# Turning the rows of an eight-expert layer by 16-bit transfers in place of matrix transposes

## The chip, the cores and the metric

The kernel runs on one core of a Trainium2 chip. A core has a matrix engine (TensorE; PE in the profile, PEld for its weight loads), VectorE (DVE), ScalarE (ACT), GpSimd (POOL) and SyncE (SP), which here only issues transfers. Each engine works through its own list of instructions in order; semaphores tie the lists together. Sixteen DMA engines move data for all of them. SBUF is the memory of 128 partitions that the engines work in, PSUM the memory that TensorE writes to. The metric is the device time of one execution in microseconds; lower is better.

## The reference

Two stages. The first is a recurrent attention with a decay per channel (4 batches, 8 heads, 768 steps, head width 48); its result is laid out as 3072 rows (tokens) of 384 channels. The second sends each row to one of eight experts, the one with the largest logit, and scales the expert's answer by its softmax weight:

```python
state = alpha[:, :, t, :, None] * state + np.einsum('bhd,bhe->bhde', k[:, :, t], v[:, :, t])
y[:, :, t] = np.einsum('bhd,bhde->bhe', q[:, :, t], state)
...
expert_idx = np.argmax(logits, axis=1)
...
h = np.maximum(x_sorted[lo:hi] @ w1[e], 0.0)      # 384 -> 1024
y_sorted[lo:hi] = h @ w2[e]                       # 1024 -> 384
...
return (gate_w[:, None] * y).astype(np.float32)
```

Everything is 32-bit floating point.

## The kernel before

**First half.** Attention runs in 24 tiles of 128 steps (6 chunks of 4 batches), in a loop written out by hand: the order of the calls in the loop over `i` (L669 to L743) is the order of the instructions on each engine. GpSimd forms the scaled keys and queries of tile `i + 2` (`operands`, L433; its output `kqb` has three buffers), carries the decay of a chunk's end to its rows (`decay_rows`, L414, tile `er`), multiplies the carried state by it (`scale_state`, L471, tile `U`) and makes some of the one-hot rows that route tokens (`one_hots`, L288). TensorE turns `er` into columns (`decay_cols`, L427), VectorE copies them (`E`, L431), and `scale_state` waits for that. TensorE's `read_state` (L480) waits for `U`. The finished rows go to a buffer `x_rows` in device memory. At `i = 21` TensorE counts the one-hots of 16 tiles together into `tok` (`tokens`, L296).

**Second half.** The experts are ordered by how many rows they have; place 0 has the most. Places have fixed capacities: 424 - 8i rows for place i, of which place 0 has 256 done early, within the first half's end. So the rows per place are 168, 416, 408, 400, 392, 384, 376, 368, in blocks of 128: 2, 4, 4, 4, 4, 3, 3, 3. For each place:

- `gather` (L787): one indirect transfer per block, issued by GpSimd, brings rows into `xg` (rows on partitions; two buffers).
- `turn` (L795): three TensorE transposes per block into PSUM (`tp`), and a copy by VectorE or ScalarE into `xgT` (channels on partitions). `row_sums` (L805) forms sums of halves on VectorE into `t1`.
- `layer1` (L863): 384 channels into 1024, by a scheme of Strassen's kind on the first two thirds of the channels: seven products P1 to P7 in place of eight, with the last third of the channels (R11, R12, R22, Rd) added plainly. It runs over four tiles `a`; `chain` (L816) holds the parts `p1`, `p2`, `p7`, `p6`, `p5`, `c22`, `p34`. P1, P6, P5 and P3 are added one after another onto one PSUM bank A, and between two of them ScalarE copies the bank out (`keep`: `p1`, `u2`, `u4`; `p` and `u` in the profile). The next product on A therefore waits for that copy. VectorE's adds and ScalarE's relus form `h`; VectorE forms sums of `h` in `th`. The third and fourth product of a tile run late, within the next tile, ahead of its fifth.
- `layer2` (L924): 1024 into 384 with the same chain, four matmuls to a product; the last third of the output channels is done plainly with eight matmuls of the full row count (L957). The results lie in `zT`, channels on partitions.
- `rows_out` (L988): three TensorE transposes per block and a ScalarE copy into `zo` (`scatter`, L972), then an indirect transfer by GpSimd to the output rows. It is a generator; `layer1` of the next place takes one block of it per tile (`next(rows, None)`, L917).

The loop over the places (L1153) sets the order: `layer1` with the previous place's results beside it; `begin`, the first product of layer 2; then the fetch of a later place's `w1` on SP, the gather of place `i + 2`, and `rest` (L953) with `between`, the generator that turns the next place's rows in two steps. The fetch of a later `w2` follows. On SP the fetches wait until the weight buffer that they overwrite has been read (two buffers). The instruction order on each engine is the program's order here too. The last place has no transposed results: `rows_layer2` (L998) leaves rows on partitions.

Of the kernel before, what the change touches and what calls it, by code (L numbers as in the profile page):

```python
# [10 lines left out]
I32 = mybir.dt.int32  # L11
AX = mybir.AxisListType.X
# [6 lines left out]
def kernel(  # L19
# [29 lines left out]
    nc = tc.nc  # L49
# [313 lines left out]
    with tc.tile_pool(name="ld", bufs=6) as ld, \  # L363
# [305 lines left out]
        for i in range(-4, NT):  # L669
# [114 lines left out]
    def blocks(g):  # L784
        return [(j, min(C, g["n"] - j * C)) for j in range(-(-g["n"] // C))]

    def gather(g):  # L787
        g["xg"] = xg_pool.tile([C, NJ, Dm], F32, name="xg")
        for j, r in blocks(g):
# [5 lines left out]
    def turn(g):  # L795
        g["xT"] = wk.tile([C, DB, CAP0], F32, name="xgT")
# [7 lines left out]

    def row_sums(g):  # L805
        m = g["n"] // 2
        g["t1"] = wk.tile([C, 5, CAP0 // 2], F32, name="t1")
# [8 lines left out]
    def chain(g, terms, out, res):  # L816
# [37 lines left out]
        def p34():  # L854
            terms(bank["A"][:, :m], False, "P3", "R12")
            res(0, 1, bank["A"][:, :m])
            terms(bank["B"][:, :m], False, "P4", "Rd")
# [3 lines left out]
        return p1, p2, p7, p6, p5, c22, p34  # L861

    def layer1(g, rows, ahead, last):  # L863
# [57 lines left out]
        ahead()  # L921
        prev()

    def layer2(g):  # L924
        n, m = g["n"], g["n"] // 2
        w2, h, s, t = g["w2"], g["h"], g["s2"], g["th"]
        g["zT"] = wk.tile([C, DB, CAP0], F32, name="zT")
# [23 lines left out]
        p1, p2, p7, p6, p5, c22, p34 = chain(g, terms, out, res)  # L951

        def rest(ahead, between):  # L953
            p2()
            d2 = mps.tile([C, 512], F32, name="pC", tag="pC")
            for f in range(FB):
                nc.tensor.matmul(  # L957
                    d2[:, :n], lhsT=w2[:, f, 2 * C :], rhs=h[:, f, :n], start=(f == 0), stop=(f == FB - 1),
                )
            ahead()  # L960
            p6()
            nc.scalar.copy(z[:, 2, :n], d2[:, :n])
# [9 lines left out]
    def scatter(g, j, r, zp, shared=False):  # L972
        zo = wk.tile([C, Dm], F32, name="zo", bufs=3)
# [3 lines left out]
        else:  # L977
            nc.scalar.copy(zo[:r], zp)  # L978
        ins = nc.gpsimd.indirect_dma_start(  # L979
# [8 lines left out]
    def rows_out(g):  # L988
        for j, r in blocks(g):
            zp = mps.tile([C, DB, C], F32, name="tp", tag="tp")  # L990
            for a in range(DB):
                nc.tensor.transpose(zp[:r, a, :], g["zT"][:, a, j * C : j * C + r], ident[:])
# [266 lines left out]
```

## Time and profile before

| | |
|---|---|
| median of 23 runs | 416.78 us (415.71 to 418.3) |
| the profiled execution: time | 416.86 us |
| its span, first to last instruction | 415.0 us |
| granted TensorE clock, mean | 0.997 |
| first half, about | 0 to 157 us |
| place 0, about | 157 to 182 us |
| place 3, both layers, about | 249.5 to 282.7 us: TensorE busy 33.1, VectorE 17.3, ScalarE 12.0, GpSimd 7.8 us |
| the last place and the end, about | 378 to 415 us |

The span is what the trace covers; the time of the execution has 1.86 us more around it. In the profile a matrix transpose is a MATMUL with the identity (`ident`) as an input. One matmul of 32-bit data is recorded as two MATMUL records, one transpose as one. Matmuls are pipelined: the durations overlap, and what one costs is seen from the starts of its successors. A line number after L is that of the kernel before. In the groups by line each row gives line, engine, operation, output and inputs, shape, count, then busy time, the mean duration in ns, and the idle time of the engine just ahead, with what ended it.

### The profile page before, as it was taken

To read this page: it belongs to the slowest core of one execution; us is meant where nothing else is said; L and a number is where in the kernel's file an instruction comes from. 1 tells how busy PE (TensorE), PEld (TensorE's weight loads), DVE (VectorE), ACT (ScalarE), POOL (GpSimd) and SP (SyncE) were. 2 spreads that over 40 slices of the span, in tenths; PEclk is the share of its full clock that TensorE was granted. 3 is DMA by queue.
4 is the path that set the end of the run, shared out by engine and by line. 5 is a ranking of instruction groups with operands and counts; after the bars stand their busy time and mean duration, and the time that the engine had idled before them with its cause. 6 is when DMAs were issued, how large, how long until landed. Compare 5 with 4: busy or idle time off the path is not lost.

```text
span 415.0 us, 9238 instructions
## 1 busy us (share of the span) xinstructions
PE 403.6 (97%) x3525; PEld 340.7 (82%) x3525; DVE 213.1 (51%) x644; ACT 170.6 (41%) x453; POOL 143.7 (35%) x193
## 2 busy tenths in 40 slices
PE   7999999999998999999999999999999999999995
PEld 4677888888887875999699889979979979979952
DVE  5545545665567574645833663463573573553200
ACT  4575555565654530134125314513513523523510
POOL 5555464596758105604002501310330230200101
PEclk9999999999999999999999999999999999999998
DMA  8999999999863217764405335155154153200101
GB/s 171 201 206 216 200 215 197 214 205 225 195 180 118 80 39 263 250 238 125 154 6 186 102 132 171 50 201 172 39 210 148 62 207 122 85 1 21 35 19 36
DMA packets 120098, 59.08 MB, mean 142 GB/s; under 512 B 102934, under 2 KB 114287, under 8 KB 120052
## 3 DMA queue, kind: packets, MB, share of 16 engines
q1 hardware_dynamic: 114932, 48.80, 44.8%
q0 software_dynamic: 3424, 9.59, 6.7%
q8 instruction: 29, 0.48, 0.5%
q10 hardware_dynamic: 1696, 0.08, 0.3%
q14 instruction: 17, 0.14, 0.1%
HBM read 48.95 MB, written 9.58 MB: 141 GB/s over the span
## 4 chain that ended last, share of the span: by engine, by line
PE 81%; issue 7%; POOL 4%; ACT 3%; DMA 2%; ACTq 1%; DVE 1%; POOLq 0%
PE pA L884 11%; PE pB L884 9%; PE pC L957 8%; PE pA L942 8%; PE pC L884 4%; PE pB L942 4%; PE sA L461 4%; PE cum L392 4%; PE tp L448 4%; PE y L498 3%; PE x L535 3%; PE pA L1096 3%; PE pC L942 2%; PE tp L800 2%; PE pA L1124 2%
## 5 line engine op out<-in xcount | busy, mean ns | idle before, releaser
L979 POOL DMA_INDIRECT out_dram<-zo,sp x25 | 27.0, 1079 | 169.9 <-ACT zo L978 114.7
L184 DVE TENSOR_TENSOR h_sb<-pB,u 128x208 f32<-128x208 f32 (+6 forms) x56 | 20.2, 361 | 60.9 <-PE pB L884 44.9
L828 ACT COPY u<-pA 128x208 f32<-128x208 f32 (+6 forms) x68 | 21.6, 318 | 54.0 <-PE pA L942 50.3
L438 POOL TENSOR_TENSOR kqb<-k_sb,icp 128x384 f32<-128x384 f32 x23 | 23.1, 1002 | 28.5 <-PE y L509 13.8
L957 PE MATMUL pC<-h_sb,w 128*128 128x416 f32 (+5 forms) x96 | 32.9, 496 | 0.0
L884 PE MATMUL pA<-t,s 128*128 128x208 f32 (+6 forms) x112 | 28.6, 337 | 0.6
L461 PE MATMUL sA<-qT,kT 48*128 48x128 f32 x192 | 27.7, 284 | 0.9 <-DVE qT L452 0.9
L790 POOL DMA_INDIRECT xg<-x_rows,gp x25 | 25.9, 1035 | 7.6 <-issue 6.1
L957 PEld LDWEIGHTS pC<-h_sb,w 128*128 128x128 f32 x96 | 18.1, 190 | 12.0 <-issue 4.4
L461 PE MATMUL sB<-qT,kT 48*128 48x128 f32 x192 | 27.7, 285 | 0.0
L884 PE MATMUL pA<-xgT,w 128*128 128x208 f32 (+6 forms) x112 | 27.7, 329 | 0.0
L461 PEld LDWEIGHTS sA<-qT,kT 48*128 48x128 f32 x192 | 23.1, 187 | 3.8 <-ACT kT L454 1.1
L448 PE MATMUL tp<-ident,kqb 128*128 128x128 f32 x192 | 25.9, 278 | 0.1
L884 PE MATMUL pB<-t,w 128*128 128x208 f32 (+6 forms) x112 | 23.4, 331 | 0.2 <-DVE h_sb L184 0.2
L438 POOL TENSOR_TENSOR kqb<-q_sb,cp 128x384 f32<-128x384 f32 x23 | 23.1, 1005 | 1.2 <-DMA q_sb<-in_q_dram 0.8
L897 ACT ACTIVATE h_sb<-h_sb 128x416 f32<-128x416 f32 (+6 forms) x28 | 14.8, 530 | 20.5 <-DVE h_sb L184 20.5
L448 PEld LDWEIGHTS tp<-ident,kqb 128*128 128x128 f32 x192 | 20.8, 140 | 3.0 <-issue 0.8
L884 PE MATMUL pC<-xgT,w 128*128 128x208 f32 (+6 forms) x112 | 23.1, 329 | 0.0
L461 PEld LDWEIGHTS sB<-qT,kT 48*128 48x128 f32 x192 | 23.1, 187 | 0.0
L542 DVE TENSOR_REDUCE lgn<-x 128x8 f32<-128x32 f32 x23 | 4.4, 191 | 35.0 <-PE x L535 30.9
L469 DVE TENSOR_TENSOR dA<-sA,cmask 128x512 f32<-128x512 f32 x24 | 16.5, 689 | 10.1 <-PE sB L461 9.9
L392 PE MATMUL cum<-lna,cum_m 128*128 128x384 f32 x48 | 21.4, 529 | 0.3
(252 smaller groups left out, 961.0 us busy)
## 6 DMA issues: line engine op xcount, KB each, us to landing
w<-in_moe_w_dram SPq DMA_DIRECT2D x14, 1536.0 KB, 7.4
x_rows<-xs SPq DMA_DIRECT2D x24, 192.0 KB, 3.6
v_sb<-in_v_dram SPq DMA_DIRECT2D x10, 384.0 KB, 5.4
k_sb<-in_k_dram SPq DMA_DIRECT2D x9, 384.0 KB, 6.1
q_sb<-in_q_dram SPq DMA_DIRECT2D x9, 384.0 KB, 5.8
a_sb<-in_alpha_dram SPq DMA_DIRECT2D x8, 384.0 KB, 3.6
a_sb<-in_alpha_dram SPq DMA_DIRECT2D x8, 192.0 KB, 3.6
w<-in_moe_w_dram SPq DMA_DIRECT2D x6, 256.0 KB, 3.1
```

The costliest lines, as they stand in the source:

```text
L184: eng.tensor_tensor(out, a, b, op=ALU.add)
L392: nc.tensor.matmul(cum[:, :Dm], lhsT=cum_m[:], rhs=st[s]["lna"][:], start=True, stop=True)
L438: eng.tensor_tensor(by_half(kq[:, i]), d[n].rearrange("s (a p) d -> s a p d", a=2), d[e][:].rearrange("s (a p d) -> s a p d", a=2, p=NP), ...
L448: nc.tensor.transpose(tp[:, p, :], pair(kqb[s % 3][:, i], p), ident[:])
L461: nc.tensor.matmul(t[:, p, :], lhsT=d["kT"][r : r + D, p, :], rhs=d["qT"][r : r + D, p, :], start=True, stop=True,)
L469: nc.vector.tensor_tensor(t[:], d["sc"][i][:], cmask[:, None, :].to_broadcast([C, NP, C]), op=ALU.mult)
L790: nc.gpsimd.indirect_dma_start(out=g["xg"][:r, j, :], out_offset=None, in_=x_d[:, :], in_offset=bass.IndirectOffsetOnAxis(ap=g["gi"](j, r) ...
L828: nc.scalar.copy(t[:, :m], bank["A"][:, :m])
L884: nc.tensor.matmul(out, lhsT=ops[n_][0], rhs=ops[n_][1], start=first and n_ == names[0], stop=True, skip_group_check=True,)
L942: nc.tensor.matmul(out, lhsT=lhs, rhs=rhs, start=first and f == 0, stop=True, skip_group_check=True)
L957: nc.tensor.matmul(d2[:, :n], lhsT=w2[:, f, 2 * C :], rhs=h[:, f, :n], start=(f == 0), stop=(f == FB - 1),)
L979: ins = nc.gpsimd.indirect_dma_start(out=out[:, :], out_offset=bass.IndirectOffsetOnAxis(ap=g["si"](j, r), axis=0), in_=zo[:r], in_offset= ...
```

## The change

1. Results (`rows_out`) and the gathered rows of places 2 to 7 (`turn`) are no longer turned by TensorE. A copy splits 32-bit words into two planes of 16-bit halves (`z_halves`, `x_halves`), a transposing transfer issued by SP turns each block, and another copy joins the halves again (`z_whole`, `x_whole`). The copies are ScalarE's, but for GpSimd's `x_halves` of place 2 and VectorE's `z_whole` of block 3. Places 0 and 1 keep `turn` for their rows.
2. `z_halves` stands where `rows_out` stood, in tiles 1 to 3 of the next layer 1 and behind its loop, now between the third and the fourth product of the previous tile. `z_whole` and the scatters move to the second layer that follows. `x_halves` of place `i + 2` stands at the end of the second layer of place `i`, `x_whole` at the start of the next one.
3. `p34` becomes `p3` and `p4`. In the first tile of a layer 1 the sixth product comes ahead of the seventh. In layer 2 the sixth comes between the halves of the third channels' eight matmuls.
4. In the first half `scale_state(i)` comes behind `operands(i + 2)` at i = 8, 12, 16 and 20.
5. Gathers fetch rows in multiples of 16; `zo` has four buffers; some tiles are a little larger; `plain` uses the buffer of `h_sb`.

```diff
-            if i % B == 0:
-                do(scale_state, i)
+            if i == B:
+                scale_state(i)
             do(operands, i + 2)
+            if i > B and i % B == 0:
+                scale_state(i)
...
+    def x_halves(g, copy=nc.scalar.copy):
+
+        g["xt"] = wk.tile([C, NJ, 2 * DB, C], U16, name="xt")
+        for j, r in blocks(g, 16):
+            t = wk.tile([C, 2, Dm], U16, name="xh", bufs=4)
+            copy(t[:r], g["xg"][:r, j, :].bitcast(U16).rearrange("p (c h) -> p h c", h=2))
+            nc.sync.dma_start(g["xt"][:, j, :, :r], t[:r].rearrange("p h c -> p (h c)"), transpose=True)
+            yield
+
+    def x_whole(g):
+        g["xT"] = wk.tile([C, DB, CAP0 + 8], F32, name="xgT")
+        to = halves(g["xT"])
+        for j, r in blocks(g):
+            nc.scalar.copy(
+                to[:, :, :, j * C : j * C + r], g["xt"][:, j].rearrange("p (h a) t -> p h a t", h=2)[:, :, :, :r],
+            )
+
+    def halves(t):
+        return t.rearrange("p a t -> p (a t)").bitcast(U16).rearrange("p (a t h) -> p h a t", h=2, a=DB)
...
-            p1, p2, p7, p6, p5, c22, p34 = tile_parts(a)
+            p1, p2, p7, p6, p5, c22, p3, p4 = tile_parts(a)
             p1()
             p2()
-            p7()
-            p6()
             if prev:
-                prev()
-            next(rows, None)
+                p7()
+                p6()
+                prev[0]()
+                next(rows, None)
+                prev[1]()
+            else:
+                p6()
+                p7()
             p5()
             c22()
-            prev = p34
+            prev = p3, p4
+        for _ in rows:
+            pass
         ahead()
-        prev()
+        prev[0]()
+        prev[1]()
...
+            third(range(FH))
+            p6()
+            next(between)
+            third(range(FH, FB))
             ahead()
-            p6()
             nc.scalar.copy(z[:, 2, :n], d2[:, :n])
-            next(between, None)
+            next(between)
             p5()
-            next(between, None)
+            next(between)
             p7()
             c22()
-            p34()
+            p3()
+            p4()
...
-    def rows_out(g):
+    def z_halves(g):
+        g["zr"] = wk.tile([C, NJ, 2 * DB, C], U16, name="zr")
+        z = halves(g["zT"])
         for j, r in blocks(g):
-            zp = mps.tile([C, DB, C], F32, name="tp", tag="tp")
-            for a in range(DB):
-                nc.tensor.transpose(zp[:r, a, :], g["zT"][:, a, j * C : j * C + r], ident[:])
-            scatter(g, j, r, zp[:r].rearrange("p a c -> p (a c)"))
+            t = wk.tile([C, 2, DB, C], U16, name="zh", bufs=4)
+            nc.scalar.copy(t[:, :, :, :r], z[:, :, :, j * C : j * C + r])
+            if r < C:
+                nc.gpsimd.memset(t[:, :, :, r:], 0)
+            nc.sync.dma_start(g["zr"][:, j], t.rearrange("p h a t -> p (h a t)"), transpose=True)
             yield
+
+    def z_whole(g, copy, *js):
+        for j, r in blocks(g):
+            if j not in js:
+                continue
+            zo = wk.tile([C, Dm], F32, name="zo", bufs=4)
+            copy(
+                zo[:r].bitcast(U16).rearrange("p (c h) -> p h c", h=2),
+                g["zr"][:r, j].rearrange("p (h a) c -> p h (a c)", h=2),
+            )
+            put(g, j, r, zo)
...
+        if i == 0:
+            for _ in x_halves(groups[2], nc.gpsimd.tensor_copy):
+                pass
...
         def turned():
-            if nxt:
+            if i == 0:
                 yield from turn(nxt)
                 row_sums(nxt)
+                return
+            z_whole(groups[i - 1], nc.scalar.copy, 0, 1)
+            yield
+            if nxt:
+                row_sums(nxt)
+            z_whole(groups[i - 1], nc.scalar.copy, 2)
+            z_whole(groups[i - 1], nc.vector.tensor_copy, 3)
+            yield
+            if i + 2 < E:
+                for _ in x_halves(groups[i + 2]):
+                    pass
+            yield
 
         between = turned()
 
+        if 0 < i < E - 1:
+            x_whole(nxt)
         if last:
+            for _ in between:
+                pass
```

`put` is the second part of `scatter`, the indirect transfer to the output rows.

More of the change, by code (lines that the diff above doesn't have):

```diff
@@ L782, with blocks @@
     mps = ctx.enter_context(tc.tile_pool(name="moe_ps", bufs=2, space=PSUM))
-    def blocks(g):
-        return [(j, min(C, g["n"] - j * C)) for j in range(-(-g["n"] // C))]
+    def blocks(g, by=1):
+        return [(j, min(C, -(-(g["n"] - j * C) // by) * by)) for j in range(-(-g["n"] // C))]
     def gather(g):
         g["xg"] = xg_pool.tile([C, NJ, Dm], F32, name="xg")
-        for j, r in blocks(g):
+        for j, r in blocks(g, 16):
             nc.gpsimd.indirect_dma_start(
@@ L926, in layer2 @@
         w2, h, s, t = g["w2"], g["h"], g["s2"], g["th"]
-        g["zT"] = wk.tile([C, DB, CAP0], F32, name="zT")
+        g["zT"] = wk.tile([C, DB, CAP0 + 8], F32, name="zT")
         z = g["zT"]
@@ L949, in res @@
                 nc.scalar.copy(out(i, k), at)
-        p1, p2, p7, p6, p5, c22, p34 = chain(g, terms, out, res)
+        p1, p2, p7, p6, p5, c22, p3, p4 = chain(g, terms, out, res)
         def rest(ahead, between):
@@ L1010, in plain @@
     def plain(g):
-        hT = wk.tile([C, FB, C], F32, name="hT")
+        hT = wk.tile([C, FB, CAP0], F32, name="h_sb")[:, :, :C]
         for f in range(FB):
@@ L1146, in beside @@
     def beside(i):
-        work = [rows_out(groups[i - 1])] + [weight_sums(groups[1], 2, nc.vector)] * (i == 1)
+        work = [z_halves(groups[i - 1])]
+        if i == 1:
+            work += [weight_sums(groups[1], 2, nc.vector)]
         while work:
```

26 lines of the change are left out of this document (16 added, 10 removed).

## The prediction

> **What bounds the kernel now.** I read the page first, then the groups by line, then the time lines of TensorE and ScalarE over one place of the second half, then the DMA rows.
>
> ```profile
> PE 403.6 (97%) x3525; PEld 340.7 (82%) x3525; DVE 213.1 (51%) x644; ACT 170.6 (41%) x453; POOL 143.7 (35%) x193
> ...
> PE 81%; issue 7%; POOL 4%; ACT 3%; DMA 2%; ACTq 1%; DVE 1%; POOLq 0%
> ```
>
> TensorE is busy in 97% of the span and holds 81% of the chain of work that ended last; ScalarE and VectorE are about half idle. Time goes down only where TensorE does less or waits less. What the change takes off it are two groups:
>
> ```profile
> L992 PE MATMUL tp<-ident,zT 128*128 128x128 f32 (+6 forms) x72 | 11.8, 273 | 0.0
> ...
> L800 PE MATMUL tp<-ident,xg 128*128 128x128 f32 (+7 forms) x81 | 11.1, 263 | 0.0
> ```
>
> Three transposes turn one block of up to 128 rows. L992 (results) has 72, 24 blocks: 2 of place 0, 4 each of places 1 to 4, 3 each of 5 and 6. L800 (gathered rows) has 81, 27 blocks: 2 of place 0, 4 of place 1, and 21 of places 2 to 7 (4+4+4+3+3+3). The change removes all 24 of the first and 21 of the second. The busy time of a group is no price for them, because matmuls overlap; the price is what their successors start later by. TensorE's time line in place 3, first layer (start, duration, line, output and inputs):
>
> ```profile
> 251.86 0.50 PE L884 MATMUL pA<-t,s 128*128 128x200 f32 x2
> 252.19 0.49 PE L992 MATMUL tp<-ident,zT 128*128 128x128 f32 x3
> 252.77 0.61 PE L884 MATMUL pA<-t,s 128*128 128x200 f32 x2
> ...
> 259.97 0.84 PE L884 MATMUL pB<-t,w 128*128 128x200 f32 x4
> 260.65 0.49 PE L992 MATMUL tp<-ident,zT 128*128 128x128 f32 x3
> 260.98 0.51 PE L884 MATMUL pA<-t,s 128*128 128x200 f32 x2
> ```
>
> Two products take 0.68 us (259.97 to 260.65), one 0.34; a block of three transposes takes 0.33 (260.65 to 260.98). In the first tile the fifth product starts 0.58 after the transposes instead: 0.25 is a wait.
>
> Second layer of the same place, where the next place's rows are turned after the sixth and the fifth product:
>
> ```profile
> 269.71 5.54 PE L957 MATMUL pC<-h_sb,w 128*128 128x400 f32 x16
> 275.08 1.52 PE L942 MATMUL pA<-th,s 128*128 128x200 f32 x8
> 276.44 0.82 PE L800 MATMUL tp<-ident,xg 128*128 128x128 f32 x6
> 277.09 1.60 PE L942 MATMUL pA<-th,s 128*128 128x200 f32 x8
> 278.53 0.77 PE L800 MATMUL tp<-ident,xg 128*128 128x128 f32 x6
> 279.23 1.62 PE L942 MATMUL pB<-th,s 128*128 128x200 f32 x8
> 280.69 1.52 PE L942 MATMUL pA<-h_sb,s 128*128 128x200 f32 x8
> ```
>
> From the sixth product to the third is 5.61 us (275.08 to 280.69); three products of four matmuls at 1.36 (275.08 to 276.44) are 4.08, so four blocks cost 1.53. For three blocks, the same stretch in the chain of waits:
>
> ```profile
> 275.25 1.35 PE pA L942 x8
> ...
> 308.03 1.33 PE pA L942 x8
> ...
> 313.07 1.33 PE pA L942 x8
> ```
>
> 313.07 - 308.03 - 3 x 1.33 = 1.05. From 275.25 to 308.03 is one place's period, 32.8 us.
>
> **The change, part by part.** *First layer.* 24 blocks x 0.33 = 7.9 us of transposes go. The wait in the first tile changes its shape. ScalarE there:
>
> ```profile
> 251.85 0.37 ACT L895 ACTIVATE h_sb<-h_sb 128x200 f32<-128x200 f32 x1 [0.77 <-DVE h_sb L184]
> 252.40 0.33 ACT L828 COPY u<-pA 128x200 f32<-128x200 f32 x1 [0.17 <-PE pA L884]
> ...
> 260.17 0.34 ACT L893 ACTIVATE h_sb<-pA 128x200 f32<-128x200 f32 x1 [0.32 <-PE pA L884]
> 261.25 0.54 ACT L897 ACTIVATE h_sb<-h_sb 128x400 f32<-128x400 f32 x1 [0.74 <-DVE h_sb L184]
> 261.69 0.46 ACT L978 COPY zo<-tp 128x384 f32<-128x384 f32 x1
> 262.05 0.33 ACT L828 COPY u<-pA 128x200 f32<-128x200 f32 x1
> ...
> 276.69 0.33 ACT L828 COPY u<-pA 128x200 f32<-128x200 f32 x1 [7.48 <-PE pA L942]
> 276.91 0.50 ACT L962 COPY zT<-pC 128x400 f32<-128x400 f32 x1
> ```
>
> The fifth product adds onto bank A and waits for the copy u of the sixth. With the sixth moved ahead of the seventh, u is no longer last behind TensorE but behind the relu (251.85): relu to about 252.15, u to 252.48, fifth product at 252.5 instead of 252.77. Without transposes it could have started at 252.2. So this tile saves about 0.28, not 0.33 + 0.25, and seven places have it: 7.9 - 7 x 0.05 = 7.6 us saved in first layers. The change's title names this reordering; by these rows it earns nearly nothing by itself.
>
> *What comes in its place on ScalarE.* A half-splitting copy has 768 16-bit elements per partition. No row has one. From 200 to 400 elements a copy grows from 0.33 to 0.50 (276.69, 276.91), 0.85 ns each; 768 give 0.81, or about 0.70 from start to start, since 261.69 to 262.05 overlaps by 0.10. Bounds: 0.35 us if two 16-bit elements went at once, 2.1 us if every other element cost threefold. I take 0.70, the rate of the nearest rows. In the first layer one such copy per tile stands between the two relus of the previous tile, where ScalarE now idles 0.74 (ahead of 261.25); the old zo copy behind it goes, so the next u comes earlier, not later. Cost nothing; beyond about 1.5 us the late second relu would hold VectorE's adds and then TensorE. VectorE's z_whole copy takes the place of two or more turning copies: nothing.
>
> *Second layer.* Places 1 to 6 turn their successor's rows: 3 x 1.53 + 3 x 1.05 = 7.7 us go. What waits next? The fifth product needs u of the sixth; now half of the third channels' eight matmuls (5.37 us, 269.71 to 275.08) stands between, 2.7 us against a copy of 0.33: hidden. ScalarE gets x_whole (2.1 to 2.5), three z_whole (2.1) and x_halves (2.1 to 2.8), at most 7.4 us in a layer of about 14.9 (7 x 1.36 + 5.37). In its order: x_whole starts after the last relu, about 1.2 us into the layer, and ends by 4.0, before the sixth product ends at 5.7. Two z_whole fit into the second half of the third channels. The zT copy, a third z_whole and the copy of the fifth product end about 0.5 after that product. x_halves then need 2.8, the copy of the third product follows, and the next copy wanted is p of the next place, three products and a matmul later (3 x 1.36 + 0.34 = 4.4): hidden with some 1 us to spare.
>
> *Transfers.* Eight per place at most (4 z, 4 x), all on SP's queue.
>
> ```profile
> x_rows<-xs SPq DMA_DIRECT2D x24, 192.0 KB, 3.6
> ...
> xg<-x_rows,gp POOLq DMA_INDIRECT x25, 5.4
> ```
> ```profile
> q1 hardware_dynamic: 66637, 16.41, 96.0%
> ```
> ```profile
> q1 hardware_dynamic: 6800, 14.16, 25.9%
> ```
>
> The nearest transfer of that size lands in 3.6 us. Of engine time: the second fence is the window 30 to 110 us, small packets: 0.96 x 80 x 16 / 66637 = 18.4 ns of one engine a packet. A block as 768 runs of 256 bytes is then 768 x 18.4 / 16 = 0.9 us of all sixteen; as 98304 single elements it is 113 us. I take 0.9 and keep both ends. The third fence is the window 216 to 378: 14.16 MB are nine weight loads, 0.259 x 162 / 9 = 4.7 us each, two a place. 8 x 0.9 + 9.3 = 16.5 in a new period of about 30.0 (32.8 - 1.53 - 3 x 0.33 - 0.28): room. Who waits: z_halves are copied over the first layer and wanted by z_whole 9 us or more later; x_halves are wanted a whole layer later, behind the last relu. Behind each transfer on SP stands a weight load whose use is 15 us off. Hidden while a transfer lands in under 9 us. On POOL the memset and the moved puts have the slack of an engine busy 35%; the four copies of place 2 there cost 768 x 2.7 ns (U below, 0.52 for 192) = 2.1 us each, over long before 201 us, where x_whole wants them. In the last place three z_whole copies and puts come behind its first layer, 2.1 us on ScalarE, where TensorE has blocks of four microseconds left: hidden.
>
> *First half.* operands moved ahead of scale_state at i = 8, 12, 16, 20.
>
> ```profile
> 55.05 1.01 POOL L418 TENSOR_TENSOR er<-er,alpha 4x384 f32<-4x384 f32 x1
> 57.07 0.52 POOL L476 TENSOR_TENSOR U<-acc,E 128x192 f32<-128x192 f32 x1 [1.00 <-DVE E L431]
> 57.55 1.00 POOL L438 TENSOR_TENSOR kqb<-k_sb,icp 128x384 f32<-128x384 f32 x1
> ...
> 124.17 0.51 POOL L476 TENSOR_TENSOR U<-acc,E 128x192 f32<-128x192 f32 x1 [2.27 <-DVE E L431]
> ```
> ```profile
> 58.23 0.65 PE L488 MATMUL y<-qT,U 48*48 48x128 f32 x16
> ```
> ```profile
> PE tok L298 <- POOL oh_c L291: 1.4, 1, 1.4
> ```
>
> At i = 8 POOL has only 1.0 us of wait to fill with two products of 1.0 each: U ends at 58.5 instead of 57.6, and TensorE's read at 58.23 is 0.3 late. At i = 20 the wait of 2.27 covers both, so the one-hots behind come 2 us earlier and TensorE's only long wait of this half, 1.4 us for the last one-hot, goes. Net -1.1 us; bounds -1.4 to +0.9.
>
> *Sum.* 7.6 + 7.7 + 1.1 = 16.4 us. The profiled execution has a span of 415.0 and a time of 416.86, 1.86 outside the span; 415.0 - 16.4 + 1.86 = 400.5, and 0.08 less against the median of 416.78: **400.4 us**.
>
> **The rivals.** *ScalarE becomes the bound in the second layer.* Against 0.70, a copy at 1.4: x_halves take 5.6, the copies behind them end some 1.7 us too late for the next place's first tile, in five places; 9 us of the gain go: 409 us, with lesser mishaps of the same kind 404 to 416. At 2.1 the copies ahead of u of the fifth product are late too (3.7 in six places), x_halves by 4.6 in five, and the first layer's relus by 0.5 in some 20 tiles: 55 us, about 455, slower. For it: no row shows 16-bit or every-other-element access. Against: ScalarE's price per element is the same for copies out of PSUM (0.33 to 0.50 for 200 more) and for relus out of SBUF (251.85 and 261.25: 0.37 to 0.54).
> The Trainium skill, "SBUF — State Buffer", section "Door 1: The DMA port swizzle", says that consecutive accesses to one 16-byte line run at full bandwidth, so that 16-bit data may be stepped up to eight elements for free. By that rule this rival is near nothing and the copies stay at 0.70; no trace of before can show it, so I leave it its chance.
>
> *The transfers become the bound; slower.* One mechanism: a turning transfer occupies the queue alone for its landing time of 3.6 us. Per place, 8 x 3.6 + 9.3 = 38.1 against 30.0, late by 8.1 once (i = 2), by 4.5 in three places with 7 transfers, by 0.9 at i = 1 with 6: 22.5 us, all of it at the z_whole and x_whole copies on ScalarE, behind which TensorE's accumulations stand: 422.9 us. With T for one, 35 T - 103.5 is lost; it decides against the change from T = 3.4 us on. For it: no row shows how a turning transfer is cut. Against: transfers of 192 KB overlap in the first half, where q1 keeps the engines 96% busy.
> The Trainium skill, "VectorE: DVE Perf Modes", section "The three transpose paths", speaks against the change: 390 ns for a 128 x 128 turn on TensorE, 1309 ns by the DMA crossbar, and it advises TensorE. Six such turns to a block would be an estimate of 7.9 us a transfer, and 35 x 7.9 - 103.5 = 173 us lost, about 573. The trace already differs on the first figure: a turn costs TensorE 0.11 us here.
>
> *The change doesn't do what it says*: the transfer falls apart into single elements, 45 x 113 us, milliseconds; in the chance of the rival before.
>
> **How the numbers follow.** Forecast, 398 to 404: 0.62. ScalarE partly the bound, 404 to 416: 0.15; threefold copies, slower: 0.03. Gains eaten to within 0.2%, about what a measurement here can tell from no change (415.9 to 417.6): 0.04. Transfers the bound, 420 and up: 0.14. Better than 398: 0.02. Faster 0.62 + 0.15 + 0.02 = 0.79, same 0.04, slower 0.17. The range 398 to 417.6 leaves out 0.19.
>
> **What would show it.** Right: no L992 group, L800 down to 18 matmuls, fifth products starting 0.34 after their forerunner, ScalarE's 16-bit copies near 0.8 us, transposing transfers landing in under 6 us, the wait of TensorE on oh_c gone, a place's period near 30.0. Wrong: TensorE waiting for u, p or h_sb behind ScalarE copies above 1.2 us, or ScalarE waiting for xt or zr.

## The result and the profile after

| | before | after |
|---|---|---|
| median | 416.74 us (415.67 to 418.3, 62 runs) | 400.62 us (399.76 to 401.9, 8 runs) |
| ratio, with its 95% interval | | 0.9613 (0.9598 to 0.9627) |
| the profiled execution: time, span | 416.86, 415.0 us | 401.68, 399.9 us |
| granted clock, mean | 0.997 | 0.996 |

The forecast was 400.4 us. The profiled execution after lies 1.06 us above its median, so the two traces show 15.1 us of the 16.1 between the medians. The traces gain 1.3 us less than the 16.4 forecast; that the median comes within 0.2 us of the forecast is in part luck.

The page of after: the busy times, then the head of the chain that ended last.

```profile
PE 388.5 (97%) x3390; PEld 326.6 (82%) x3390; DVE 207.2 (52%) x636; ACT 219.3 (55%) x502; POOL 147.2 (37%) x203
...
POOL 0%; POOLq 0%
```

TensorE has 135 fewer instructions, 45 blocks of three transposes, and is still busy in 97% of a shorter span. ScalarE went from 41% to 55%. The chain of this trace breaks off at the last instruction and can't be used; I read the time lines instead. TensorE's time line, first rows of stretches of the kernel: of before the early second layer and place 1, of after the same two and the second layers of places 1 to 4:

```profile
155.44 8.01 PE L1096 MATMUL pA<-w,h 128*128 128x384 f32 x24 [0.47 <-ACT h L631]
...
181.87 0.52 PE L884 MATMUL pA<-xgT,w 128*128 128x208 f32 x2
```
```profile
154.52 4.78 PE L1152 MATMUL pA<-w,h 128*128 128x384 f32 x14 [0.47 <-ACT h L632]
182.41 0.51 PE L909 MATMUL pA<-xgT,w 128*128 128x208 f32 x2
196.86 1.57 PE L974 MATMUL pA<-h_sb,w 128*128 128x208 f32 x8
228.27 1.54 PE L974 MATMUL pA<-h_sb,w 128*128 128x204 f32 x8
259.12 1.52 PE L974 MATMUL pA<-h_sb,w 128*128 128x200 f32 x8
289.43 1.49 PE L974 MATMUL pA<-h_sb,w 128*128 128x196 f32 x8
```

The differences of such starts cut the span into nine segments, which all later readings use. A period "1 to 2" runs from the second layer of place 1 to that of place 2. The forecast's share is put together from its own terms (for a period with four blocks 1.53 + 4 x 0.33 - 0.05).

| segment | before | after | difference | forecast |
|---|---|---|---|---|
| up to the early second layer | 155.44 | 154.52 | -0.92 | -1.1 |
| place 0 | 26.43 | 27.89 | +1.46 | 0 |
| place 1, first layer | 15.31 | 14.45 | -0.86 | -0.61 |
| 1 to 2 | 34.65 | 31.41 | -3.24 | -2.80 |
| 2 to 3 | 33.54 | 30.85 | -2.69 | -2.80 |
| 3 to 4 | 32.96 | 30.31 | -2.65 | -2.80 |
| 4 to 5 | 32.09 | 29.76 | -2.33 | -2.32 |
| 5 to 6 | 31.17 | 29.21 | -1.96 | -1.99 |
| the rest | 53.41 | 51.50 | -1.91 | -1.99 |
| sum | 415.0 | 399.9 | -15.1 | -16.4 |

(Spans are known to 0.1 us, so the rest to 0.05.) Every segment but one is within 0.45 us of its forecast; place 0 went the other way. The copies that took over, in the groups by line of after:

```profile
L1046 ACT COPY zo<-zr 128x768 uint16<-128x768 uint16 (+2 forms) x20 | 20.0, 1052 | 0.0
L821 ACT COPY xgT<-xt 128x768 uint16<-128x768 uint16 (+5 forms) x21 | 17.5, 929 | 0.0
L1035 ACT COPY zh<-zT 128x768 uint16<-128x768 uint16 (+6 forms) x24 | 17.1, 714 | 0.0
L813 ACT COPY xh<-xg 128x768 uint16<-128x768 uint16 (+2 forms) x17 | 12.9, 833 | 0.0
...
L813 POOL COPY xh<-xg 128x768 uint16<-128x768 uint16 (+1 forms) x4 | 3.1, 824 | 0.0
L803 PE MATMUL tp<-ident,xg 128*128 128x128 f32 (+2 forms) x18 | 2.5, 263 | 0.0
L1046 DVE COPY zo<-zr 32x768 uint16<-32x768 uint16 (+3 forms) x4 | 2.4, 588 | 0.0
```

The means of L821 and L1035 hold short last blocks too. L803 keeps its 18 transposes of places 0 and 1; the group of the results is gone. Their place on ScalarE, in its time line over the end of place 3:

```profile
263.03 2.97 ACT L821 COPY xgT<-xt 128x768 uint16<-128x768 uint16 x4
267.92 0.33 ACT L851 COPY u<-pA 128x200 f32<-128x200 f32 x1 [1.92 <-PE pA L974]
268.14 1.98 ACT L1046 COPY zo<-zr 128x768 uint16<-128x768 uint16 x2
270.60 0.49 ACT L1000 COPY zT<-pC 128x400 f32<-128x400 f32 x1 [0.49 <-PE pC L991]
270.99 1.06 ACT L1046 COPY zo<-zr 128x768 uint16<-128x768 uint16 x1
271.92 0.32 ACT L851 COPY u<-pA 128x200 f32<-128x200 f32 x1
272.12 2.30 ACT L813 COPY xh<-xg 128x768 uint16<-128x768 uint16 x3
274.61 0.33 ACT L981 COPY zT<-pA 128x200 f32<-128x200 f32 x1 [0.18 <-PE pA L974]
```

The copies of TensorE's banks (u, zT, at 267.92, 270.60 and 274.61) still wait for TensorE and not it for them: there is room, but the last gap is only 0.18. The u at 271.92 stands behind a joining copy; TensorE's next product on that bank starts in time even so (273.06, 1.36 behind its forerunner). The new transfers, in the page's list of issues (count, median us to landing), then the row of SP's queue in the window 210 to 360 us:

```profile
zr<-zh SPq DMA_TRANSPOSE x24, 2.8
xt<-xh SPq DMA_TRANSPOSE x21, 3.8
```
```profile
q1 hardware_dynamic: 34000, 20.87, 55.1%
```

In the same window of before, q1 had 6800 packets and 28.0%. Thirty-six turning transfers start in it: (34000 - 6800) / 36 = 756 packets each and (0.551 - 0.280) x 150 / 36 = 1.1 us of all sixteen engines.

### The profile page after: what moved, and what is told of

The parts are those of the page before. It is cut to its first block, busy times and chain, and to the rows that moved or that the text cites. A ratio compares the mean times of both kernels' runs of the same rounds, so it can differ in the third digit from the quotient of the medians.

```text
span 399.9 us, 9032 instructions
## 1 busy us (share of the span) xinstructions
PE 388.5 (97%) x3390; PEld 326.6 (82%) x3390; DVE 207.2 (52%) x636; ACT 219.3 (55%) x502; POOL 147.2 (37%) x203
## 5 line engine op out<-in xcount | busy, mean ns | idle before, releaser
L1021 POOL DMA_INDIRECT out_dram<-zo,sp x25 | 26.0, 1039 | 137.5 <-ACT zo L1046 127.0
L991 PE MATMUL pC<-h_sb,w 128*128 128x416 f32 (+5 forms) x96 | 33.9, 496 | 0.0
L793 POOL DMA_INDIRECT xg<-x_rows,gp x25 | 24.3, 972 | 6.9 <-issue 6.8
L518 ACT COPY yT<-y 128x512 f32<-128x512 f32 x24 | 14.1, 586 | 18.6 <-PE y L510 8.6
L920 ACT ACTIVATE h_sb<-h_sb 128x208 f32<-128x208 f32 (+6 forms) x28 | 10.3, 366 | 25.2 <-DVE h_sb L185 25.2
```

What stands on the lines that cost most here:

```text
L518: nc.scalar.copy(d["yT"][:], y[:, :, : 2 * C].rearrange("r g (j t) -> r g j t", j=2))
L793: nc.gpsimd.indirect_dma_start(out=g["xg"][:r, j, :], out_offset=None, in_=x_d[:, :], in_offset=bass.IndirectOffsetOnAxis(ap=g["gi"](j, r) ...
L920: nc.scalar.activation(out(0, 0), out(0, 0), AF.Relu)
L991: nc.tensor.matmul(d2[:, :n], lhsT=w2[:, f, 2 * C :], rhs=h[:, f, :n], start=(f == 0), stop=(f == FB - 1),)
L1021: ins = nc.gpsimd.indirect_dma_start(out=out[:, :], out_offset=bass.IndirectOffsetOnAxis(ap=g["si"](j, r), axis=0), in_=zo[:r], in_offset= ...
```

## The experiments

Twelve kernels ran in three sets, each set on a chip beside the kernel before. That kernel took 421.34, 422.10 and 423.00 us there, with more scatter than above; in the traces of this section the extra time lies ahead of place 1. So I give the ratio to before, and read the segments; from place 1 on those repeat to 0.02 us in nearly all kernels that leave them alone. Differences "to after" are to the segments in the table above. Line numbers shift by a few between the kernels.

**1. Results turned by TensorE again** (no 16-bit copies and transfers for them):

```
-        work = [z_halves(groups[i - 1])]
+        work = [rows_out(groups[i - 1])]
...
-            z_whole(groups[i - 1], nc.scalar.copy, 0, 1)
-            z_whole(groups[i - 1], nc.scalar.copy, 2)
-            z_whole(groups[i - 1], nc.vector.tensor_copy, 3)
```

> The changed kernel, with the results of the places turned by TensorE again, at the place where the splitting copies stood; the gathered rows still by transfers. Theory (TensorE's time is the sum of what it issues, ScalarE's copies are hidden): 24 blocks x 0.33 us come back, 7.9 us, 400.6 to 408.5 us. Rival (ScalarE or the transfers hold something back in the changed kernel, so that taking 20 joining and 24 splitting copies off ScalarE pays): less than 6 us come back.

Ratio 0.9821 (0.9776 to 0.9867). Seven segments from place 1 on: +0.65, +1.32, +1.19, +1.16, +1.14, +0.80, +1.46, together +7.7 us to after. Up to place 6 a block costs 0.27 to 0.33 us. In the rest TensorE issues 0.99 us more, and 0.4 lies behind its last matmul. So this half of the change is worth about 24 x 0.30, 7.3 us on TensorE, close to its price, and the rival (less than 6 us) is out.

**2. Gathered rows turned by TensorE again:**

```
-            for _ in x_halves(groups[i + 2]):
-                pass
...
-            x_whole(nxt)
...
+                tn = turn(nxt)
+                next(tn)
...
+                next(tn, None)
```

> The changed kernel, with the gathered rows of places 2 to 7 turned by TensorE again, in the second layer, the results still by transfers. Theory: 21 blocks come back, 6.9 us at 0.33 a block or 7.7 by the stretch measured in the kernel before; GpSimd's four copies in place 0 go with it, and with them TensorE's wait of 1.05 us there, so 5.5 to 6.7 us net: 406.1 to 407.3 us. Rival (that wait has nothing to do with GpSimd's copies): 6.9 to 7.7 us, 407.5 to 408.3.

Ratio 0.9887 (0.9829 to 0.9946); segments 0, +2.14, +2.54, +2.63, +2.75, +2.82, +0.83, together +13.7 us: nearly twice what was expected. TensorE's waits between 205 and 345 us in this kernel (waiting line, releaser, us in total, times, longest):

```profile
PE pB L974 <- DVE zT L185: 2.4, 2, 1.5
PE pB L974 <- DVE t L188: 0.8, 1, 0.8
PE pA L909 <- ACT u L851: 0.4, 1, 0.4
```

Neither before nor after has any such wait listed in that window. My kernel put turning copies and joining copies of both schemes on the same engines, and VectorE's sums (`zT`) came late. The transposes explain 7.7; of the other 6.0 these rows explain 3.6, and the rest stays open. The run prices a mixture, not the undone half alone.

**3. The new order of products alone, in the kernel before** (sixth ahead of seventh in a first tile; sixth among the third channels):

```
+                p6()
+                p7()
...
+                if f == FH:
+                    p6()
```

> The kernel before with the new order of products alone: sixth ahead of seventh in the first tile, sixth between the third channels' halves; all transposes stay on TensorE. Theory (the copy u of the sixth product is ready 0.24 us earlier, since it then waits for the relu and not for the sixth product): 7 x 0.24 = 1.7 us less than before, 415.1. Rival (the order is worth nothing): 416.7.

Ratio 0.995 (0.9919 to 0.998): half a per cent faster by itself. Segments against before: -0.31, -0.38, -0.37, -0.35, -0.33, -0.33, -0.31, together -2.4 us. Of each, 0.25 to 0.31 lies in the first layer and 0.07 to 0.09 in the second.

**4. The change with the old order in the first tile** (`p7` ahead of `p6`):

```
+                p7()
                 p6()
-                p7()
```

> The changed kernel with the old order in the first tile: seventh product, then sixth. Theory: u then comes 0.2 us after the sixth product's end and the fifth starts 2.61 us after the tile's first instead of 2.33, 0.28 in each of 7 places: 2.0 us slower than the changed kernel, 402.6. Rival, as the prediction has it (by itself the reordering earns nearly nothing): 400.6.

Ratio 0.9691 (0.9651 to 0.9731); segments +0.30, +0.40, +0.29, +0.28, +0.26, +0.25, +0.10, together +1.9 us. TensorE's first tile of place 3 in this kernel, then in after:

```profile
250.12 0.50 PE L909 MATMUL pA<-xgT,w 128*128 128x200 f32 x2
...
252.72 0.60 PE L909 MATMUL pA<-t,s 128*128 128x200 f32 x2 [0.41 <-ACT u L851]
```
```profile
245.19 0.50 PE L909 MATMUL pA<-xgT,w 128*128 128x200 f32 x2
...
247.52 0.60 PE L909 MATMUL pA<-t,s 128*128 128x200 f32 x2
```

From the tile's start to the fifth product it is 2.60 us with the old order and no transposes, 2.33 with the new one. Before, with transposes, it was 2.61: there the transposes of a first tile lay inside the wait for u. Without the reordering, removing them would have gained nothing in that tile.

**5 and 6. Who splits place 2's rows.** In 5 ScalarE, within place 0's second layer; in 6 two blocks GpSimd and two ScalarE. The edit of 5 (6 changes the engine of two of the four):

```
-        if i == 0:
-            for _ in x_halves(groups[2], nc.gpsimd.tensor_copy):
-                pass
...
+            xh = x_halves(groups[2])
             ahead(1)
             rest_layer2(g, 0)
             next(between)
+            next(xh), next(xh)
```

> The changed kernel with the four splitting copies of place 2 moved from GpSimd to ScalarE, two behind each of the first two parts of place 0's second layer. Theory (GpSimd's copies hold VectorE up: one of its instructions of 0.18 us took 2.86 us beside them, and TensorE then waited 1.05 us for VectorE's relu): that instruction is back at 0.2 us, place 0 takes 26.4 us instead of 27.9, and the time falls by 1.0 to 1.5 us to 399.1 to 399.6. Rival (VectorE was held by a transfer or by its own queue): no change, 400.6.

> As the run before, but two of the four copies stay on GpSimd. Theory: VectorE is held half as long, some 1.3 us instead of 2.7, which its slack takes in: TensorE's wait in place 0 is under 0.3 us, and the time is that of the run before within 0.4. Rival (GpSimd's copies and VectorE's delay are unrelated): the instruction still takes 2.5 us or more, or 0.2.

Ratios 0.9534 (0.9494 to 0.9573) and 0.96 (0.9569 to 0.9631). All segments from place 1 on are those of after in both, but for 0.1 at the end; place 0 takes 29.07 and 32.67. In 5 none of VectorE's short instructions is long any more, as expected; its place 0 can't be held against the 26.4 us expected, since on this chip run 3 takes 31.67. In 6 one of 0.14 us takes 2.04 beside the two copies, TensorE waits 1.0 us for VectorE, and place 0 is 3.6 us longer than in 5: the expectation of a wait under 0.3 us and a time within 0.4 failed. But the 3.6 us aren't the copies' alone. In 6 the granted clock is 0.50 for 6.8 us of place 0, which costs half of that, 3.4 us (an estimate); in 5 it is 1.00 throughout. What kernel 5 removes is seen in after itself. The time lines of VectorE (one line of before, then after), GpSimd and TensorE in place 0:

```profile
173.59 0.18 DVE L1084 SCALAR_TENSOR_TENSOR xx<-xx,kx 128x24 f32<-128x24 f32 x1
```
```profile
172.67 2.86 DVE L1140 SCALAR_TENSOR_TENSOR xx<-xx,kx 128x24 f32<-128x24 f32 x1
175.45 0.32 DVE L1169 TENSOR_SCALAR h_sb<-pB 128x168 f32<-128x168 f32 x1
```
```profile
173.12 3.12 POOL L813 COPY xh<-xg 128x768 uint16<-128x768 uint16 x4
```
```profile
175.83 0.55 PE L1180 MATMUL pA<-h_sb,w 128*128 128x168 f32 x2 [1.05 <-DVE h_sb L1169]
```

An instruction on 24 elements is recorded at 2.86 us; before it took 0.18. It stands beside GpSimd's four copies. Behind it on VectorE stands h_sb, and TensorE waits 1.05 us for that.

**7. ScalarE's splitting copies of the gathered rows made twice:**

```
+            for _ in range(2 if copy == nc.scalar.copy else 1):
+                copy(t[:r], g["xg"][:r, j, :]...)
```

> The changed kernel with each of ScalarE's splitting copies of gathered rows made twice, 4 more in places 1 and 2 and 3 more in places 3 to 5, 0.77 us each. Theory (ScalarE has about half a microsecond to one to spare behind them, then the copies of the next place's first tile come late and TensorE's fifth product waits): about 2.6 us lost in places 1 and 2, 1.1 in 3 to 5, 7 to 8.5 us in all, 408 to 409. Rival (ScalarE, busy in 55% of the span, takes them in): under 1 us.

Ratio 0.9799 (0.9751 to 0.9847); the periods 1 to 2 to 5 to 6: +3.61, +3.64, +0.49, +0.59, +0.71, together +9.0 us. TensorE's waits between 205 and 345 us:

```profile
PE pA L910 <- ACT p L852: 3.4, 3, 2.0
PE pA L910 <- ACT zT L982: 2.1, 1, 2.1
```

The copy p of place 2's first tile, in ScalarE's time line of after, then the product that waits for it in this kernel, and a slice of this kernel behind that wait (length, then busy us and instructions of TensorE, its loads, VectorE, ScalarE and GpSimd, the granted clock, the DMA share, GB/s):

```profile
214.68 0.33 ACT L851 COPY p<-pA 128x204 f32<-128x204 f32 x1 [1.09 <-PE pA L909]
```
```profile
222.34 0.61 PE L910 MATMUL pA<-t,s 128*128 128x204 f32 x2 [2.05 <-ACT p L852]
```
```profile
225.00:227.00 2.00, 2.00 (x7) 1.96 (x7) 0.37 (x1) 0.49 (x2) 0.00 (x0) 0.50 0.85 231
```

In after, with four blocks copied once, p still waits 1.09 us for TensorE: that is ScalarE's room. With the copies doubled TensorE waits 2.05 us for p. Behind that wait the granted clock is 0.50 for 3.4 us, and again behind the other long wait; nowhere else from place 1 to place 6. So of the 3.6 us lost where four blocks are copied twice, about 2.0 are the wait and 1.7 the clock (half of 3.4 us, an estimate); where three are, 0.5 to 0.7 are lost at full clock. The bound that the first rival named is real; at the measured durations it isn't reached.

**8. The old order of operands and state in the first half:**

```
-            if i == B:
-                scale_state(i)
+            if i % B == 0:
+                do(scale_state, i)
             do(operands, i + 2)
-            if i > B and i % B == 0:
-                scale_state(i)
```

> The changed kernel with the first half as before: scale_state ahead of operands in every chunk. Theory: TensorE's wait of 1.36 us for the last one-hot is back, the 0.3 to 0.5 us lost at i = 8 are not: 0.9 us slower, 401.5. Rival (what was gained at i = 20 is lost again in the wait for the early rows behind it): 400.6.

Ratio 0.9713 (0.9662 to 0.9764). TensorE's wait for the last one-hot (`oh_c`) is back, 1.4 us. The reads of the state at `i = 21` and 22, ahead of and behind the token count, in TensorE's time line of this kernel and of after:

```profile
129.67 0.66 PE L489 MATMUL y<-qT,U 48*48 48x128 f32 x16
136.29 0.66 PE L489 MATMUL y<-qT,U 48*48 48x128 f32 x16
```
```profile
129.78 0.65 PE L489 MATMUL y<-qT,U 48*48 48x128 f32 x16
134.84 0.66 PE L489 MATMUL y<-qT,U 48*48 48x128 f32 x16
```

6.62 against 5.06 us: 1.56 us hang on this order, where 0.9 net was expected. The other distances from the third read on, `i = 8` among them, are those of the changed kernel in the later set to 0.02 us.

**9, 10 and 11, beside the changed kernel again.** The changed kernel unaltered:

> The changed kernel itself, unaltered, beside which the three others of this set are read. Both theories: ratio to before 0.961 give or take 0.006; from place 1 on every segment repeats to within 0.1 us of the first profile of after (place 1's first layer 14.45; places 31.41, 30.85, 30.31, 29.76, 29.21; end 51.5). If VectorE is held by GpSimd's four 16-bit copies, one short instruction of VectorE in place 0 (0.14 to 0.18 us by itself) is recorded at 2 to 3 us beside them.

Ratio 0.9644 (0.9598 to 0.969). From place 1 on 14.44, 31.41, 30.86, 30.31, 29.76, 29.21, 51.61: the same as the first profile. Place 0 takes 33.45. The long VectorE instruction is 0.63 us only (a product that takes 0.14 by itself), so this part of the expectation failed: VectorE stood until 174.75, two of GpSimd's 3.1 us from 172.75 on were over.

*u ahead of the relu* in the first tile:

```
-            res(0, 0)
+            if relu:
+                res(0, 0)
...
+                relu(h[:, a, :m])
```

> In the first tile of a layer 1 the relu of the first quarter goes behind the copy u of the sixth product, so that this copy no longer stands behind the relu on ScalarE. If the relu is what the fifth product waits for there (my reading of the first tile: 2.33 us where six products would be 2.04), each of the seven first layers loses 0.25 to 0.3 us: segments of places 1 to 5 shorter by about 0.29 each, 1.8 to 2.0 us in all, about 0.995 of after. Rival: the relu only moves the wait, to the third product or to the sum of h that VectorE forms behind it: segments the same within 0.1.

Ratio 0.9607 (0.9562 to 0.9653), 404.98 against 406.64 us for the changed kernel beside it; the intervals overlap. The segments don't: -0.37, -0.32, -0.38, -0.37, -0.36, -0.35, -0.36, together -2.5 us to the changed kernel of the same set. The first tile of place 3:

```profile
248.90 0.50 PE L910 MATMUL pA<-xgT,w 128*128 128x200 f32 x2
...
250.94 0.51 PE L910 MATMUL pA<-t,s 128*128 128x200 f32 x2
```

Six products in 2.04 us, six times 0.34, with no wait left. The rival (a moved wait) is out.

*Three readings together* (u ahead of the relu, ScalarE for place 2, and the state first at `i = 8` too):

```
-            if i == B:
+            if i in (B, 2 * B):
                 scale_state(i)
```

> Three of the readings in one kernel: u ahead of the relu (the run before); the halves of place 2's rows copied by ScalarE within place 0's second layer, not by GpSimd; and the operands ahead of the scaled state only from i = 12 on, so not at i = 8. If the three readings hold and add up: place 0 shorter than after by 1.0 to 1.5 us, the later segments by 0.29 each as in the run before, the first half by 0.2 to 0.4, together 3 to 4 us, ratio to after 0.991. Rival: ScalarE is short in place 0 and gives back what VectorE gains there: 0.995, as u alone.

Ratio 0.9586 (0.9536 to 0.9636), 404.64 us: 0.3 less than with u alone, which these intervals can't tell from nothing, and 2.0 less than the changed kernel, not the 3 to 4 expected. From place 1's second layer on the segments are those of the run before; place 1's first layer takes 14.52, 0.45 more than there. Place 0 takes 31.74, 1.7 less than in the changed kernel of this set, but the clock alone makes that difference: it is 0.50 for 3.4 us of place 0 here and for 6.8 there. The part up to the early second layer takes 157.48, 3.3 more. There TensorE waits 2.8 us for the logarithms (`lna`), which no edit touches, where the changed kernel waits 0.9, and the clock is 0.50 for another 3.4 us. Around `i = 8` it gains nothing: 5.88 from read to read, 5.89 in the changed kernel beside it.

*GpSimd's four copies made twice:*

```
+            for _ in range(2 if copy == nc.gpsimd.tensor_copy else 1):
+                copy(t[:r], g["xg"][:r, j, :]...)
```

> GpSimd's four copies of place 2's halves are each made twice, into the same tile. If GpSimd's copies hold VectorE while they run, the short VectorE instruction beside them grows from 1.8 to 2.9 us to about 5 to 6 us, and place 0 grows by 2 to 3.5 us against after in the same set. Rival, if the long instruction is a quirk of the record or is due to the gathers: it stays at 3 us or below and place 0 changes by under 0.5 us. Segments from place 1 on the same in both.

Ratio 0.9692 (0.963 to 0.9754); place 0 takes 34.01, +0.56. VectorE and GpSimd in place 0:

```profile
171.49 0.79 DVE L1120 TENSOR_TENSOR_SCAN ve<-nb,zero_e 128x8 f32<-128x8 f32 x1
...
173.33 0.97 DVE L1127 TENSOR_TENSOR xb<-vb,kx 128x192 f32<-128x192 f32 x1
174.23 0.34 DVE L1131 TENSOR_REDUCE xx<-xa 128x24 f32<-128x192 f32 x1
...
175.06 0.73 DVE L1134 CAST xi<-xx 1x24 int32<-1x24 f32 x1
...
176.79 0.77 DVE L1138 SCALAR_TENSOR_TENSOR vb<-first,vb 128x8 f32<-128x8 f32 x1
177.59 0.36 DVE L1139 TENSOR_TENSOR xb<-xb,vb 128x192 f32<-128x192 f32 x1
```
```profile
171.41 7.23 POOL L814 COPY xh<-xg 128x768 uint16<-128x768 uint16 x8
```

Not one instruction of 5 to 6 us, as expected, but many shorter ones. From the start of the scan to that of L1139 it is 6.10 us; the same stretch takes 2.24 us in before, where no copy runs beside it. VectorE lost 3.9 us within 7.2 us of copies. The theory holds in its direction and its form was wrong: here each is held for less than one copy (about 0.9 us), where in after one was held for about three. Place 0 doesn't grow by the 2 to 3.5 us expected, since most of that loss lies beside another wait: VectorE stands still until 171.24 here and until 174.75 in the changed kernel of this set, and the two start the instruction of L1139 at 177.59 and 177.72. From place 1 on the segments are those of that kernel, but for 0.37 more in 2 to 3 and 0.2 less at the end, which stay unexplained.

## Why the prediction was right

*The two prices held.* 0.33 us for three transposes in a first layer and 1.53 or 1.05 for a second layer's blocks came from starts of successors, not from busy times; with them the forecast of the seven later segments is 15.3 us, and 15.6 was measured. Run 1 confirms the first price alone (7.3 us on TensorE of 7.9). Run 2 doesn't confirm the second alone, since it added waits of its own, but the traces before and after do: cut at the starts of the first layers as well, the second layers of places 1 to 6 are shorter by 1.96, 1.41, 1.38, 1.09, 1.05 and 1.23 us, against 1.53 three times and 1.05 three times. (By run 3, 0.07 to 0.09 of each is the sixth product's new place.) In place 1 there was also a wait of TensorE for VectorE's `h_sb` before, a product starting 0.77 us behind its forerunner (at 199.70) where 0.35 is usual; it is gone in after, and that is the 0.44 by which 1 to 2 beat its forecast.

*The first tile* is right in size and wrong in its reading. The fifth product was forecast 2.33 us behind the tile's start, with u behind the relu, and stands there (245.19 to 247.52). But "by these rows it earns nearly nothing by itself" is wrong: runs 3 and 4 show 2.4 us (some 2 of it in first layers) and 1.9 us. The failed step is the comparison: I set the reordering against a tile with neither transposes nor a wait, where I should have asked what the tile does without it. Runs 4 and 9 answer: 2.60 without it, 2.33 with it, 2.04 with the relu out of the way too.

*ScalarE's copies.* 0.70 us from start to start was taken for all of them. Measured is 0.74 for the splitting of gathered rows ((2.30 - 0.83) / 2, by the rows at 272.12 and of L813), and 0.93 for joining (1.98 - 1.05, at 268.14), a term mis-sized by a third. The cover, "some 1 us to spare", was right: ScalarE waits 1.09 us ahead of the next place's p with four blocks to split; run 7 shows where it ends. The rival with copies of 1.4 us had the right mechanism. That it priced 9 us for them and run 7, with the splittings of gathered rows at twice their length, lost 9.0 is luck: the rival had 1.7 us in each of five places, run 7 lost 3.6 in two of them, nearly half of it by the clock, and 0.5 to 0.7 in three.
By the rule from the Trainium skill that the prediction weighed, "SBUF — State Buffer", section "Door 1: The DMA port swizzle", every other 16-bit element is free. The trace agrees for reading (0.83 us recorded, 0.81 by count) and not for writing (1.05 us).

*The transfers.* 768 runs of 256 bytes and 0.9 us of engine time were forecast, 756 packets and 1.1 us measured; landing under 6 us, measured 2.8 and 3.8. No row of TensorE's or ScalarE's waits in the window 205 to 345 us names `zr` or `xt`. The slower rival decides against the change from 3.4 us of the queue for each; gathered rows took 3.8 to land and nothing was lost, so a turn doesn't occupy the queue alone while it lands.
By the Trainium skill, "VectorE: DVE Perf Modes", section "The three transpose paths", with 1309 ns for one turn, six turns to a block would be an estimate of 7.9 us. A block landed in 2.8 or 3.8 us, so the measurement differs and decides.

*First half.* Forecast -1.4 at `i = 20` and +0.3 at `i = 8`. Measured: 1.56 (run 8), and TensorE's wait for `oh_c` is gone. At `i = 8` the profile of after shows 6.59 us from read to read against 6.20 before, the forecast loss, but in the later sets it is 5.88 in either order: it depends on where GpSimd stands when it gets there.

*What failed: place 0*, +1.46 us where nothing was forecast. The step is "the four copies of place 2 there cost ... 2.1 us each, over long before 201 us". Their size was wrong to the good side (3.12 us for the four), and when they end was never the question. What they hold up is VectorE beside them, and through it TensorE. From the start of the early second layer to the transposes behind the wait for `h_sb` it is 21.70 us in after (154.52 to 176.22) and 20.38 in before (155.44 to 175.82): 1.3 of the 1.46 us lie there. In all nine traces with GpSimd's copies some short VectorE instruction beside them is recorded at 0.6 to 2.9 us in place of 0.14 to 0.18; in none of the five without (before, 2, 3, 5, 10). Each of these ends 0.01 to 0.04 us behind the end of one of GpSimd's copies, in after behind the third of the four; the products of 192 elements that are held end 0.2 behind one. That leaves little room for another cause.
On the later chips place 0 takes 32.2 to 34.2 us with the copies and 29.1 to 31.7 without, but more than half of that difference is the clock. It is 0.50 for 3.4 or 6.8 us of place 0 in all of these traces but run 5. With half of that time taken off (an estimate) place 0 takes 29.3 to 31.0 us with the copies and 29.0 to 30.0 without.
The Trainium skill, "SBUF — State Buffer", section "Who interferes with whom", has the rule: a VectorE instruction with two inputs in SBUF contends with a GpSimd instruction that reads SBUF; the ports that they share are an exclusive lock, and whoever issues first has it for the whole instruction while the other is blocked. The trace agrees on which instructions are held: the products, the scan and the three-operand instructions are long, the reduction among them (0.34) isn't. On the order it is less clear: in after the held instruction is recorded as starting at 172.67, 0.45 us ahead of the first copy, and it lasts to the end of the third. The conversion (0.73, by itself 0.17) has one input; the Trainium skill, in the same section, counts conversions among those that can enter a mode with the same conflict, which no run here tells apart.

*What stays open.* On the later chips VectorE and ScalarE stand still in place 0 in front of relus whose products TensorE has long finished: in the changed kernel of the last set VectorE for 6.01 us until 174.75 and ScalarE for 4.01 until 174.82. Run 3, with none of the new copies, has the same (VectorE for 5.22 until 174.39). TensorE then waits for them, and behind such waits the clock falls. A slice of the changed kernel of the last set, its columns as in run 7:

```profile
177.00:183.00 6.00, 5.50 (x20) 5.02 (x21) 4.79 (x13) 0.78 (x2) 3.67 (x4) 0.50 0.97 308
```

In run 5, whose place 0 is the shortest of the later traces, TensorE waits 1.56 and 0.56 us and the clock stays at 1.00, so what lowers it isn't shown. What VectorE and ScalarE wait for isn't settled either. So it stays open how much of place 0's time GpSimd's copies cost on those chips; shown there is that they lengthen VectorE's instructions.

## What to carry to other kernels

Price an instruction that is taken from the bounding engine by the starts of its successors, and ask for each wait beside it what else would still fill that time: transposes inside a wait are free, and removing them gains nothing until the wait goes too. When work moves to an engine that is half idle, list what runs beside it on the engines that share something with it, not only when it ends. Before two kernels' times are compared, compare the granted clock stretch by stretch: 3.4 of the 3.6 us between runs 5 and 6 in place 0 are clock, not copies. Two edits that look like one (the reordering and the transfers) are separated in two runs: each alone.

## What the runs showed of the hardware

- GpSimd copies hold VectorE: an instruction of 0.18 us took 2.86 beside four copies in after, and 3.9 us were lost over several beside eight. The held instructions end within 0.04 us of the end of a copy, held products of 192 elements 0.2 behind it.
- A ScalarE copy of 768 16-bit elements per partition takes 0.83 us with every other element on the reading side and 1.05 with it on the writing side; VectorE's joining copy, on 32 partitions or fewer, takes 0.59, GpSimd's splitting copy 0.82.
- A transposing transfer of a block (128 rows of 384 words as 16-bit halves) lands in 2.8 us from results and 3.8 from gathered rows, in 756 packets and 1.1 us of the engines.
- The granted clock can halve within a run: to 0.50 for 3.4 us twice in run 7, each time behind a wait of TensorE of about 2 us, and for 3.4 or 6.8 us in place 0 of eleven of the twelve later traces.
